# Handing work between engines at the seam of two stages, and splitting weights earlier in each unit of the last one

## The chip, the core and the metric

The kernel runs on one core of a Trainium2 chip. The metric is device time of one launch in microseconds, lower is better. Engines, as the profile names them: PE (TensorE matmul), DVE (VectorE), ACT (ScalarE), POOL (GpSimd), SP (the queue that starts most loads). Each engine works through its own list of instructions in order; semaphores tie the lists together.

## The reference

Three stages in one function: windowed attention, a mixture of 8 experts with the two best of each token, and a dense layer with a gated activation. All in float32; x has 1536 rows of 512.

```python
a = softmax(where(is_sink | in_window, q k^T / 8, -1e9));  x = a v       # 2 x 8 heads, 768 x 64
top2 = the two largest of x @ w_gate + softplus(x @ w_noise) * noise      # 8 experts
out[mask] += top2_w[mask, k, None] * (relu(x[mask] @ w1[e]) @ w2[e])      # 512 -> 1024 -> 512
h = x @ w_in                                                             # 512 -> 2048
sp = log1p(exp(h));  g = h * tanh(sp);  return g @ w_out                  # 2048 -> 512
```

## The kernel before

A float32 product is made of three fast products: each operand is split into a high part (`wh`, `xh`, `gh`) and the rest (`wl`, `xl`, `gl`), and PE adds high*high, high*rest and rest*high. A **split** of one 128x512 slice of weights is two instructions: ACT copies the staged slice to `wh` (L538), then POOL, or DVE if `lo='dve'` is given, subtracts it to make `wl` (L542). `Weights.split()` takes the next slice of a fixed list. Slices are loaded by SP into three staging buffers (`stg`); a subtraction that ends a staging buffer lets the next load start.

**Experts (`moe`).** For expert e, `l1` makes the hidden layer and `l2(e,b,half)` the output of row block b, in four blocks of two halves, with one split behind each half. An expert's rows go out to the table `yd`, and `gather(t,k)` fetches, with POOL's indirect DMA, the rows that belong to tile t of 128 tokens for choice k. Behind the last expert's halves the table `X2S` puts the **mixing** of the first four tiles: `x2a(t)` (L670, L671) scales the second gathered tile by its weight and adds the first times its own; both run on DVE, though `by='act'` sends the scaling to ACT (L669). `x2b(t)` transposes the mixed tile on PE (L676) and splits it into `xh` (ACT, L678) and `xl` (DVE, L679), the input of the last stage.

**Dense layer (`moe2`).** It runs in 48 units u: group g of 512 tokens, block f of 128 hidden columns. First come blocks 0 to 2 of group 0, each in two halves of 256 tokens; tiles 2 and 3 are transposed between the first half of block 0 and that of block 1 (`XH`). Then each unit holds, in this order: a mixing or a transposing of a later tile where the tables `XA2` and `XB2` name the unit (for the next group's tiles, so in units 0 to 31 only), `l1` (12 matmuls of 512 columns into `h`), the activation in three steps on three successive units as `MORD` says, one split in units 3 to 18 (`SPM`), a gather in even units, and `l2` of the block four units back (12 matmuls into the four banks of `o`).

The activation of block f: `mish_a` in unit f (ACT exponential L703; DVE L704, L705, L706; L706 is also the last reader of the PSUM tile `h`), `mish_b` in unit f+1 (ACT L709, L710, then the **gate**: POOL's product L711), `mish_c` in unit f+2 (ACT copy `gh` L715, DVE `gl` L716). The tiles `u` and `q` have three buffers, so unit u's exponential waits for `gl` of unit u-3. Block 3's `h` lies in a bank that the first `l2` needs as its fourth.

The order of the work is that of the code: no scheduler moves anything.

Of the kernel before, what the change touches and what calls it, by code (L numbers as in the profile page):

```python
# [467 lines left out]
    nc.scalar.activation(u,u,AF.Exp,scale=-1.0)  # L468
    nc.gpsimd.tensor_tensor(q,q,u,op=ALU.mult)
TX={(True,0,0): (0,),(True,0,1): (1,),(True,1,0): (2,),(True,2,0): (3,),(False,2,0): (0,1),(False,2,1): (2,3)}  # L470
X2S={(2,0):(lambda a,b: a(0),lambda a,b: a(1)),(3,0):(lambda a,b: b(0),lambda a,b: b(1),lambda a,b: a(2),lambda a,b: a(3))}
DS=4; LAG2=4; MB=3; GB=3; NH=3; XH=(0,0); SPM={u:1 for u in range(3,19)}; XA2=(1,5,9,12); XB2=(5,8,11,14); MORD=((0,0),(2,2),(1,1)); D_=512; FF=1024; F2=2048

class Weights:

# [71 lines left out]
def moe(ctx, tc, I, st, W, out, C=448, dbg=None, W32=None):  # L547
# [3 lines left out]
    pool=lambda name,bufs,**k: ph.enter_context(tc.tile_pool(name=name,bufs=bufs,reuse_waits="tile",**k))  # L551
# [19 lines left out]
    def l1(e,f,c0=0,c1=C,skip=0):  # L571

        xh,xl=XT[e]; n=4*e+f//4; wh,wl=W.hi[n],W.lo[n]; fs=slice(128*(f%4),128*(f%4)+128)
        p=bank['a'].tile([128,512],F32,name='a')
        w=c1-c0; i=0
        for k in range(4):
            for a,b in ((wh,xh),(wh,xl),(wl,xh)):
                nc.tensor.matmul(p[:,:w],a[:,k,fs],b[:,k,c0:c1],start=(i==0),stop=(i==11)); i+=1  # L578

        if c0==0: HH[f],HL[f]=one.tile([128,C+S],F32R,name=f'hh{f}'),one.tile([128,C-S],F32R,name=f'hl{f}')  # L580
        r=short(e); t=r+S
        for a,b in seg(c0+skip,c1,t): nc.scalar.activation(high(e,f,a,b),p[:,a-c0:b-c0],AF.Relu)
        for a,b in seg(c0+skip,c1,r,t):
            hl=HH[f][:,a+S:b+S] if r<=a<t else HL[f][:,a:b] if b<=r else HL[f][:,a-S:b-S]
            nc.vector.scalar_tensor_tensor(hl,p[:,a-c0:b-c0],0.0,high(e,f,a,b).bitcast(F32),op0=ALU.max,op1=ALU.subtract)  # L585
# [4 lines left out]
    def dbuf(t):  # L590
        if t<3: return dec.tile([128,256,2],U32,name='d64',bufs=3).rearrange("p n w -> p (n w)").bitcast(F32)
        return dec.tile([128,2,256],F32,name='dh').rearrange("p a n -> p (a n)")
    yw=st['yw']={}
    def l2(e,b,half):
        o,m=blocks(e)[b]
        if half==0: Y[0]=bank['c'].tile([128,512],F32,name='c')
        p=Y[0]
        two=0<m==S
        for f in range(4*half,4*half+4):
            n=4*e+2+f//4; wh,wl=W.hi[n][:,f%4,:],W.lo[n][:,f%4,:]  # L600
            if two:

                for i,w in enumerate((wh,wl)): nc.tensor.matmul(p[:2*m],HH[f][:,o:o+2*m],w,start=f+i==0,stop=f==7 and i==1)  # L603
            else:
                d=o-S if o>short(e) else o
                for i,(h,w) in enumerate(((high(e,f,o,o+m),wh),(high(e,f,o,o+m),wl),(HL[f][:,d:d+m],wh))): nc.tensor.matmul(p[:m],h,w,start=f+i==0,stop=f==7 and i==2)  # L606
        if half==1:
            s=yo.tile([128,512],F32,name='ys')
            if two:
                r=yo.tile([128,512],F32,name='ys')  # L610
                nc.scalar.activation(r[:m],p[m:2*m],AF.Copy)
                nc.vector.tensor_tensor(s[:m],p[:m],r[:m],op=ALU.add)
            else: nc.scalar.activation(s[:m],p[:m],AF.Copy)
            yw[e,b]=(nc.sync if (e,b)==(7,nb-1) else nc.scalar).dma_start(st['y'][e*C+o:e*C+o+m,:],s[:m])
# [17 lines left out]
    for e in range(8):  # L632
        if e: 
            
            for f in range(8):
                l1(e,f); W.split(); W.dstep(DS)
                if e<7 and f<nb: load_x(e+1,f)
                if e==7 and f>3: gather(f-4,0)
        for b in range(nb):
            if e==0 and b==LXB:  # L640
                for c in range(2,nb): load_x(0,c)
            if e==0 and b==2:
                
                for f in range(8):
                    l1(0,f,C-M,C,2*M-C); W.split(); W.dstep(2)
                    if f<nb: load_x(1,f)
            for half in range(2):
                l2(e,b,half)
                if e==0 and b==1 and half==0:
                    for c in range(2,nb): trans_x(0,c)  # L650
                if (e,half)==(7,1) and b<2: gather(2*b,1,dbuf(2*b)); gather(2*b+1,1,dbuf(2*b+1))
                W.split()
                if e==7:
                    for f in X2S.get((b,half),()): f(x2a,x2b)
                W.dstep(DS)
                for c in TX.get((e>0,b,half),()) if e<7 else (): trans_x(e+1,c)
# [25 lines left out]
def moe2(ctx, tc, I, st, W, out, C=448, dbg=None):  # L682
    nc=tc.nc; ident=st['ident']
    ph=ctx.enter_context(ExitStack())
    pool=lambda name,bufs,**k: ph.enter_context(tc.tile_pool(name=name,bufs=bufs,reuse_waits="tile",**k))
    xt=pool('n_x',1); gp=pool('n_g',GB); tp=pool('n_t',MB)
    ps_o=pool('np_o',4,space=PS); ps_h=pool('np_h',3,space=PS); ps_t=pool('np_t',1,space=PS)
    gather,x2a,x2b=st['gather'],st['x2a'],st['x2b']; X2=st['X2']; st['xt2'],st['ps_x2']=xt,lambda: (ps_t.tile([128,512],F32,name='xt') if O else ps_o.tile([128,512],F32,name='o')).rearrange("p (k q) -> p k q",k=4)
    G={}; HP={}; O={}

    e10=math.exp(10.0)
    def l1(g,f,c=slice(0,512)):
        xh,xl=X2[g]; n=32+f//4; wh,wl=W.hi[n],W.lo[n]; fs=slice(128*(f%4),128*(f%4)+128)
        if c.start==0: HP[g,f]=ps_h.tile([128,512],F32,name='h2') if (g,f)!=(0,3) else ps_o.tile([128,512],F32,name='o')
        p=HP[g,f]; i=0
        for k in range(4):
            for a,b in ((wh,xh),(wh,xl),(wl,xh)):
                nc.tensor.matmul(p[:,c],a[:,k,fs],b[:,k,c],start=(i==0),stop=(i==11)); i+=1  # L698
    Q={}
    def mish_a(g,f):  # L700
        p=HP.pop((g,f))
        u,q=[tp.tile([128,512],F32,name=n) for n in 'uq']; Q[g,f]=u,q
        nc.scalar.activation(u,p,AF.Exp)  # L703
        nc.vector.tensor_scalar(u,u,e10,None,op0=ALU.min)  # L704
        nc.vector.scalar_tensor_tensor(q,u,2.0,u,op0=ALU.add,op1=ALU.mult)  # L705
        nc.vector.tensor_tensor(u,p,q,op=ALU.mult)  # L706
    def mish_b(g,f):
        u,q=Q[g,f]
        nc.scalar.activation(q,q,AF.Ln,bias=st['two'])  # L709
        nc.scalar.activation(q,q,AF.Exp,scale=-1.0)  # L710
        nc.gpsimd.tensor_tensor(u,u,q,op=ALU.mult)  # L711
    def mish_c(g,f):
        u=Q.pop((g,f))[0]
        gh=gp.tile([128,512],F32R,name='gh'); gl=gp.tile([128,512],F32R,name='gl'); G[g,f]=(gh,gl)
        nc.scalar.activation(gh,u,AF.Copy)  # L715
        nc.vector.tensor_tensor(gl,u,gh.bitcast(F32),op=ALU.subtract)  # L716
    def l2(g,f):
        gh,gl=G.pop((g,f)); n=36+f//4; wh,wl=W.hi[n],W.lo[n]; k=f%4
        if f==0: O[g]=[ps_o.tile([128,512],F32,name='o') for _ in range(4)]
        for i in range(4):  # L720
            s=slice(128*i,128*i+128)
            for j,(a,w) in enumerate(((gh,wh),(gh,wl),(gl,wh))):
                nc.tensor.matmul(O[g][i],a[:,s],w[:,k,:],start=(f==0 and j==0),stop=(f==15 and j==2))  # L723
        if f==15:
            for i in range(4):
                if i%2==0: oo=W.spool.tile([128,2,512],F32,name='stg')
                o=oo[:,i%2,:]
                if i%2==0: nc.scalar.activation(o,O[g][i],AF.Copy)
                else: nc.vector.tensor_copy(o,O[g][i])
                r=512*g+128*i  # L730
                nc.sync.dma_start(out[r:r+128,:],o)
    
    gq=[(t,k) for t in range(4,12) for k in range(2)]
    for _ in range(2): gather(*gq.pop(0))
    for f in range(NH):
        l1(0,f,slice(0,256))
        for t in (2,3):
            if f==XH[t-2]: x2b(t)
    for f in range(NH): l1(0,f,slice(256,512))
    for u in range(48+LAG2):  # L740
        g,f=divmod(u,16)
        if g<2:
            if f in XA2: x2a(4*g+4+XA2.index(f))
            if f in XB2: x2b(4*g+4+XB2.index(f))
        if NH<=u<48: l1(g,f)
        for k,z in MORD:
            if 0<=u-k<48: (mish_a,mish_b,mish_c)[z](*divmod(u-k,16))
        if u<48:
            for i in range(SPM.get(u,0)): W.split(lo='dve' if i else 'pool')
            if f%2==0 and gq: gather(*gq.pop(0))  # L750
        if u>=LAG2: l2(*divmod(u-LAG2,16))
    ph.close()
# [79 lines left out]
```

## Time and profile before

| what | value |
|---|---|
| time, median of 3 runs | 748.19 us (747.0 to 750.71) |
| the profiled execution | 744.71 us, of which the span of the trace is 742.9 us |
| PE busy | 706.3 us, 95% |
| DVE busy | 491.1 us, 66% |
| ACT busy | 375.7 us, 51% |
| POOL busy | 352.3 us, 47% |
| chain that ended last | PE 64%, DVE 16%, DMA 6%, ACT 5% |

The last unit of the experts ends at about 459 us of the span, and the dense layer takes the rest, some 284 us. A busy share is an average over stages: what counts for an edit is where PE stood idle in the stretch that the edit touches, and which instruction released it.

### The profile page before, as it was taken

The page shows a single profiled execution, that of the slowest core. Times are in us where ns is not written, and L with a number is a line of the kernel's source. Part 1 is how long each engine was busy: PE and PEld are TensorE (multiplying, and loading weights), DVE is VectorE, ACT ScalarE, POOL GpSimd, SP SyncE. Part 2 cuts the span into 40 slices and gives each one's busy share as a digit, 9 for nine tenths or more (in the row PEclk, how much of TensorE's full clock was granted, in tenths as well). Part 3 has the DMA queues.
Part 4 walks back from the last instruction along what each step waited for, and adds up shares of the span by engine and source line. Part 5 has one row for each costly group of instructions (what it writes and reads, how often), then busy time and mean ns, then how long its engine had stood idle before and what let it go on. Part 6 is the DMA issues. An engine that isn't in the chain of part 4 may idle for free.

```text
span 742.9 us, 11343 instructions
## 1 busy us (share of the span) xinstructions
PE 706.3 (95%) x3888; PEld 591.1 (80%) x3888; DVE 491.1 (66%) x1099; ACT 375.7 (51%) x834; POOL 352.3 (47%) x321
## 2 busy tenths in 40 slices
PE   5998969999999999999999998999999999999996
PEld 4776658888788888989888886878778888888885
DVE  5778756588688788879876126689855655444442
ACT  5887633454454545545544443465545444444342
POOL 6236360575355445545445467366755442332321
PEclk9999979999999999999999999999999999999999
DMA  8995334587677778867867456212202100010001
GB/s 272 340 348 201 121 144 131 209 262 234 241 233 239 238 227 267 283 213 251 241 210 249 135 176 198 63 53 86 84 16 86 29 15 16 1 56 1 0 1 61
DMA packets 68336, 115.68 MB, mean 156 GB/s; under 512 B 6640, under 2 KB 20976, under 8 KB 68272
## 3 DMA queue, kind: packets, MB, share of 16 engines
q1 hardware_dynamic: 59424, 94.48, 39.2%
q0 software_dynamic: 3840, 12.59, 4.9%
q10 hardware_dynamic: 5008, 7.83, 3.0%
q8 instruction: 32, 0.52, 0.3%
q14 instruction: 32, 0.26, 0.1%
HBM read 82.36 MB, written 32.51 MB: 155 GB/s over the span
## 4 chain that ended last, share of the span: by engine, by line
PE 64%; DVE 16%; DMA 6%; ACT 5%; issue 3%; POOL 3%; another core or an unknown queue 1%; ACTq 1%; SPq 0%; POOLq 0%; DVEq 0%
PE o L723 15%; PE a L578 14%; PE h L698 14%; PE c L606 13%; ACT p L97 3%; PE c L603 2%; DMA wi<-dh 2%; DVE q L705 2%; DVE dh L508 2%; DVE dh L510 1%; PE a L94 1%; PE a L560 1%; POOL xg L212 1%; DVE gl L716 1%; DVE dh L506 1%
## 5 line engine op out<-in xcount | busy, mean ns | idle before, releaser
L542 POOL TENSOR_TENSOR wl<-stg,wh 128x512 fp32r<-128x512 f32 x156 | 206.4, 1335 | 171.7 <-ACT wh L538 160.6
L711 POOL TENSOR_TENSOR u<-u,q 128x512 f32<-128x512 f32 x48 | 79.0, 1645 | 146.6 <-DVE u L706 95.8
L538 ACT ACTIVATE wh<-stg 128x512 fp32r<-128x512 f32 x160 | 99.4, 625 | 39.9 <-DMA stg<-in_w_dram 12.3
L578 PE MATMUL a<-xl,wh 128*128 128x448 f32 (+1 forms) x288 | 100.1, 348 | 0.6 <-DVE xl L562 0.6
L578 PE MATMUL a<-xh,wh 128*128 128x448 f32 (+1 forms) x288 | 100.1, 348 | 0.0
L578 PE MATMUL a<-xh,wl 128*128 128x448 f32 (+1 forms) x288 | 99.9, 347 | 0.0
L703 ACT ACTIVATE u<-h 128x512 f32<-128x512 f32 x47 | 28.1, 598 | 121.4 <-PE h L698 101.7
L704 DVE TENSOR_SCALAR u<-u 128x512 f32<-128x512 f32 x48 | 22.2, 462 | 95.9 <-ACT u L703 95.8
L606 PE MATMUL c<-wh,hh 128*128 128x512 f32 x192 | 77.7, 405 | 0.0
L723 PE MATMUL o<-wl,gh 128*128 128x512 f32 x192 | 75.3, 392 | 1.7 <-POOL wl L542 1.6
L698 PE MATMUL h<-xh,wh 128*128 128x512 f32 (+1 forms) x200 | 76.9, 384 | 0.0
L606 PE MATMUL c<-wh,hl 128*128 128x512 f32 x192 | 75.5, 393 | 1.5 <-DVE hl L585 1.5
L723 PE MATMUL o<-wh,gl 128*128 128x512 f32 x192 | 74.9, 390 | 1.3 <-DVE gl L716 1.3
L698 PE MATMUL h<-xh,wl 128*128 128x512 f32 (+1 forms) x200 | 76.0, 380 | 0.0
L698 PE MATMUL h<-xl,wh 128*128 128x512 f32 (+1 forms) x200 | 76.0, 380 | 0.0
L723 PE MATMUL o<-wh,gh 128*128 128x512 f32 x192 | 74.9, 390 | 0.7 <-DVE u L706 0.7
L606 PE MATMUL c<-wl,hh 128*128 128x512 f32 x192 | 74.8, 390 | 0.0
L506 DVE TENSOR_SCALAR dh<-dh 128x256 f32<-128x256 f32 x64 | 41.6, 650 | 35.9 <-ACT dh L504 35.9
L504 ACT ACTIVATE dh<-d 128x256 f32<-128x256 f32 x64 | 27.6, 431 | 65.8 <-DMA wo<-dh 28.3
L578 PEld LDWEIGHTS a<-xl,wh 128*128 128x128 f32 x288 | 54.3, 189 | 4.7 <-DVE xl L562 1.2
L578 PEld LDWEIGHTS a<-xh,wh 128*128 128x128 f32 x288 | 54.3, 189 | 3.5
L578 PEld LDWEIGHTS a<-xh,wl 128*128 128x128 f32 x288 | 54.3, 189 | 3.3
(182 smaller groups left out, 1454.1 us busy)
## 6 DMA issues: line engine op xcount, KB each, us to landing
stg<-in_w_dram SPq DMA_DIRECT2D x64, 512.0 KB
d<-in_w_in_dram SPq DMA_DIRECT2D x32, 256.0 KB
d<-in_w_out_dram SPq DMA_DIRECT2D x32, 256.0 KB
xg<-zero SPq DMA_DIRECT2D x8, 896.0 KB
xr<-xg SPq DMA_DIRECT2D x24, 256.0 KB
yd<-ys ACTq DMA_DIRECT2D x23, 256.0 KB
wi<-dh SPq DMA_DIRECT2D x32, 128.0 KB
wo<-dh SPq DMA_DIRECT2D x32, 128.0 KB
```

Source lines behind the costliest of these rows:

```text
L97: nc.scalar.activation(o,tt[:,:n],AF.Exp,bias=NB[t][:,h:h+1],scale=-1.0,accum_out=RS[t][:,h:h+1])
L504: nc.scalar.activation(h,H,AF.Abs,scale=65536.0)
L506: h=T[i][1]; nc.vector.tensor_scalar(h,h,lo,hi,op0=ALU.max,op1=ALU.min)
L538: if hi=='act': s.nc.scalar.activation(h,src,AF.Copy)
L542: (s.nc.gpsimd if lo=='pool' else s.nc.vector).tensor_tensor(s.lo[n][:,j,:],s.stg[n,j//2][:,j%2,:],s.hi[n][:,j,:].bitcast(F32),op=ALU.subt ...
L578: nc.tensor.matmul(p[:,:w],a[:,k,fs],b[:,k,c0:c1],start=(i==0),stop=(i==11)); i+=1
L606: for i,(h,w) in enumerate(((high(e,f,o,o+m),wh),(high(e,f,o,o+m),wl),(HL[f][:,d:d+m],wh))): nc.tensor.matmul(p[:m],h,w,start=f+i==0,stop= ...
L698: nc.tensor.matmul(p[:,c],a[:,k,fs],b[:,k,c],start=(i==0),stop=(i==11)); i+=1
L703: nc.scalar.activation(u,p,AF.Exp)
L704: nc.vector.tensor_scalar(u,u,e10,None,op0=ALU.min)
L711: nc.gpsimd.tensor_tensor(u,u,q,op=ALU.mult)
L723: nc.tensor.matmul(O[g][i],a[:,s],w[:,k,:],start=(f==0 and j==0),stop=(f==15 and j==2))
```

## The change

Five things change, all between the last expert's third row block and the end of unit 31. (1) The four splits behind the last expert's blocks 2 and 3 make their `wl` on DVE instead of POOL. (2) Tiles 2 and 3 are scaled by ACT instead of DVE. (3) The first mixing of each group moves from unit 1 to unit 4 of the group, the second from 5 to 6. (4) The first transposing moves from unit 5 to 6. (5) In each unit the split is written ahead of the activation's steps instead of behind them; the gather keeps its place behind both.

```diff
-X2S={(2,0):(lambda a,b: a(0),lambda a,b: a(1)),(3,0):(lambda a,b: b(0),lambda a,b: b(1),lambda a,b: a(2),lambda a,b: a(3))}
-DS=4; LAG2=4; MB=3; GB=3; NH=3; XH=(0,0); SPM={u:1 for u in range(3,19)}; XA2=(1,5,9,12); XB2=(5,8,11,14); MORD=((0,0),(2,2),(1,1)); D_=512; FF=1024; F2=2048
+X2S={(2,0):(lambda a,b: a(0),lambda a,b: a(1)),(3,0):(lambda a,b: b(0),lambda a,b: b(1),lambda a,b: a(2,'act'),lambda a,b: a(3,'act'))}
+DS=4; LAG2=4; MB=3; GB=3; NH=3; XH=(0,0); SPM={u:1 for u in range(3,19)}; XA2=(4,6,9,12); XB2=(6,8,11,14); MORD=((0,0),(2,2),(1,1)); D_=512; FF=1024; F2=2048
@@ moe, behind each half of l2
-                W.split()
+                W.split(lo='dve' if e==7 and b>1 else 'pool')
@@ moe2, in each unit
         if NH<=u<48: l1(g,f)
+        if u<48:
+            for i in range(SPM.get(u,0)): W.split(lo='dve' if i else 'pool')
         for k,z in MORD:
             if 0<=u-k<48: (mish_a,mish_b,mish_c)[z](*divmod(u-k,16))
         if u<48:
-            for i in range(SPM.get(u,0)): W.split(lo='dve' if i else 'pool')
             if f%2==0 and gq: gather(*gq.pop(0))
```

At the seam, on DVE, before (`d_5286` and `d_5288` are the second rows of tiles 0 and 1, `d_5318` and `dh` those of tiles 2 and 3; `xl<-a` belongs to tiles 0 and 1, `xl<-o` to tiles 2 and 3):

```order
L612 TENSOR_TENSOR ys<-c,ys 64x512
L670 TENSOR_SCALAR d_5286<-d_5286,wB 128x512
L671 SCALAR_TENSOR_TENSOR xr<-xr,wA,d_5286 128x512
L670 TENSOR_SCALAR d_5288<-d_5288,wB 128x512
L671 SCALAR_TENSOR_TENSOR xr<-xr,wA,d_5288 128x512
L679 TENSOR_TENSOR xl<-a,xh 128x4x128 x2
L670 TENSOR_SCALAR d_5318<-d_5318,wB 128x512
L671 SCALAR_TENSOR_TENSOR xr<-xr,wA,d_5318 128x512
L670 TENSOR_SCALAR dh<-dh,wB 128x512
L671 SCALAR_TENSOR_TENSOR xr<-xr,wA,dh 128x512
L679 TENSOR_TENSOR xl<-o,xh 128x4x128 x2
```

and now:

```order
L612 TENSOR_TENSOR ys<-c,ys 64x512
L542 TENSOR_TENSOR wl_5340<-stg,wh_5339 128x512
L670 TENSOR_SCALAR d_5286<-d_5286,wB 128x512
L671 SCALAR_TENSOR_TENSOR xr<-xr,wA,d_5286 128x512
L670 TENSOR_SCALAR d_5288<-d_5288,wB 128x512
L671 SCALAR_TENSOR_TENSOR xr<-xr,wA,d_5288 128x512
L542 TENSOR_TENSOR wl_5340<-stg,wh_5339 128x512 x2
L679 TENSOR_TENSOR xl<-a,xh 128x4x128 x2
L671 SCALAR_TENSOR_TENSOR xr<-xr,wA,d_5318 128x512
L671 SCALAR_TENSOR_TENSOR xr<-xr,wA,dh 128x512
L542 TENSOR_TENSOR wl_5340<-stg,wh_5339 128x512
L679 TENSOR_TENSOR xl<-o,xh 128x4x128 x2
```

Four subtractions came to DVE, one of them ahead of the first mixing and two ahead of the first `xl`, and the two scalings of tiles 2 and 3 went to ACT.

On POOL from the same seam into unit 3, before (`wl4_5268` is the split just ahead of the four, `wl2_5340` the four, `wl5_5597` that of unit 3, under another number below; `u<-u,q` is the gate's product of blocks 0, 1 and 2, `xr<-yd` a gather):

```order
L666 DMA dh_5320<-yd_89,sloty_86 128x512
L542 TENSOR_TENSOR wl4_5268<-stg_5250,wh4_5267 128x512
L542 TENSOR_TENSOR wl2_5340<-stg_5292,wh2_5339 128x512 x2
L542 TENSOR_TENSOR wl2_5340<-stg_5324,wh2_5339 128x512 x2
L666 DMA xr_5443<-yd_89,sloty_86 128x512
L666 DMA xr_5445<-yd_89,sloty_86 128x512
L666 DMA xr_5542<-yd_89,sloty_86 128x512
L711 TENSOR_TENSOR u_5536<-u_5536,q_5537 128x512
L711 TENSOR_TENSOR u_5546<-u_5546,q_5547 128x512
L666 DMA xr_5568<-yd_89,sloty_86 128x512
L711 TENSOR_TENSOR u_5555<-u_5555,q_5556 128x512
L542 TENSOR_TENSOR wl5_5597<-stg_5364,wh5_5596 128x512
```

and now:

```order
L666 DMA dh_5320<-yd_89,sloty_86 128x512
L542 TENSOR_TENSOR wl4_5268<-stg_5250,wh4_5267 128x512
L666 DMA xr_5443<-yd_89,sloty_86 128x512
L666 DMA xr_5445<-yd_89,sloty_86 128x512
L666 DMA xr_5542<-yd_89,sloty_86 128x512
L711 TENSOR_TENSOR u_5536<-u_5536,q_5537 128x512
L711 TENSOR_TENSOR u_5544<-u_5544,q_5545 128x512
L666 DMA xr_5566<-yd_89,sloty_86 128x512
L542 TENSOR_TENSOR wl5_5582<-stg_5364,wh5_5581 128x512
L711 TENSOR_TENSOR u_5553<-u_5553,q_5554 128x512
```

The four subtractions are gone from between the gathers, and unit 3's stands ahead of block 2's product instead of behind it, as each unit's does up to unit 18.

On DVE in units 0 and 1, before (`h_5447` and `h_5474` are the PSUM tiles of blocks 0 and 1, `xr` the two gathered halves of tile 4):

```order
L705 SCALAR_TENSOR_TENSOR q<-u 128x512
L706 TENSOR_TENSOR u<-h_5447,q 128x512
L670 TENSOR_SCALAR xr<-xr,wB 128x512
L671 SCALAR_TENSOR_TENSOR xr<-xr,wA 128x512
L704 TENSOR_SCALAR u<-u 128x512
L705 SCALAR_TENSOR_TENSOR q<-u 128x512
L706 TENSOR_TENSOR u<-h_5474,q 128x512
```

and now:

```order
L705 SCALAR_TENSOR_TENSOR q<-u 128x512
L706 TENSOR_TENSOR u<-h_5447,q 128x512
L704 TENSOR_SCALAR u<-u 128x512
L705 SCALAR_TENSOR_TENSOR q<-u 128x512
L706 TENSOR_TENSOR u<-h_5474,q 128x512
```

The pair of tile 4's mixing left the place between blocks 0 and 1; it stands in unit 4 now, behind `gl` of block 1.

## Rows read from the trace of the kernel before

**Rows 1.** PE's waits from 455 us to the end: us in total, times, longest.

```profile
PE o L676 <- DVE xr L671: 3.0, 2, 2.4
PE o L723 <- POOL wl L542: 1.6, 2, 1.2
PE o L723 <- DVE gl L716: 1.3, 1, 1.3
PE o L723 <- DVE u L706: 0.7, 1, 0.7
```

**Rows 2.** Busy time by stretch, PE alone: length, busy (count), granted clock, DMA share, GB/s.

```profile
464.90:468.31 3.41, 3.41 (x19) 0.50 0.79 253
```

**Rows 3.** PE's timeline at the seam: start, length, instruction, idle before it.

```profile
455.52 1.03 PE L676 MATMUL a<-ident,xr 128*128 128x128 f32 x8
...
459.15 0.28 PE L698 MATMUL h<-xh,wh 128*128 128x256 f32 x1
...
460.46 0.28 PE L698 MATMUL h<-xh,wl 128*128 128x256 f32 x1
...
473.55 0.40 PE L698 MATMUL o<-xh,wh 128*128 128x512 f32 x1
```

**Rows 4.** DVE's timeline at the seam.

```profile
453.66 0.75 DVE L671 SCALAR_TENSOR_TENSOR xr<-xr,wA,d 128x512 f32<-128x512 f32 x1
456.81 1.29 DVE L679 TENSOR_TENSOR xl<-a,xh 128x512 fp32r<-128x512 f32 x2 [2.40 <-ACT xh L678]
458.01 4.26 DVE L670 TENSOR_SCALAR d<-d,wB 128x512 f32<-128x512 f32 x1
```

**Rows 5.** POOL's timeline at the seam.

```profile
454.76 0.95 POOL L666 DMA_INDIRECT dh<-yd,sloty  x1 [0.30 <-issue]
455.73 6.25 POOL L542 TENSOR_TENSOR wl<-stg,wh 128x512 fp32r<-128x512 f32 x5
```

**Rows 6.** DMA issues from 444 to 535 us: count, us to landing.

```profile
dh<-yd,sloty POOLq DMA_INDIRECT x1, 3.8
```

**Rows 7.** ACT's timeline at the seam.

```profile
456.19 1.07 ACT L678 ACTIVATE xh<-a 128x512 fp32r<-128x512 f32 x2
459.35 0.60 ACT L613 ACTIVATE ys<-c 128x512 f32<-128x512 f32 x1 [2.09 <-PE c L606]
```

**Rows 8.** DVE's timeline in units 0 to 3.

```profile
473.36 0.48 DVE L670 TENSOR_SCALAR xr<-xr,wB 128x512 f32<-128x512 f32 x1
...
479.36 1.55 DVE L716 TENSOR_TENSOR gl<-u,gh 128x512 fp32r<-128x512 f32 x1
481.63 0.43 DVE L704 TENSOR_SCALAR u<-u 128x512 f32<-128x512 f32 x1 [0.72 <-ACT u L703]
...
482.82 0.69 DVE L706 TENSOR_TENSOR u<-o,q 128x512 f32<-128x512 f32 x1
```

**Rows 9.** POOL's timeline there.

```profile
479.09 1.27 POOL L711 TENSOR_TENSOR u<-u,q 128x512 f32<-128x512 f32 x1 [2.84 <-ACT q L710]
```

**Rows 10.** DVE's timeline in units 8 and 9.

```profile
513.44 3.61 DVE L705 SCALAR_TENSOR_TENSOR q<-u 128x512 f32<-128x512 f32 x1
...
517.69 0.68 DVE L716 TENSOR_TENSOR gl<-u,gh 128x512 fp32r<-128x512 f32 x1
```

**Rows 11.** POOL's timeline in units 8 to 11.

```profile
513.95 1.30 POOL L711 TENSOR_TENSOR u<-u,q 128x512 f32<-128x512 f32 x1
515.20 1.29 POOL L542 TENSOR_TENSOR wl<-stg,wh 128x512 fp32r<-128x512 f32 x1
...
525.61 1.30 POOL L711 TENSOR_TENSOR u<-u,q 128x512 f32<-128x512 f32 x1
526.86 1.26 POOL L542 TENSOR_TENSOR wl<-stg,wh 128x512 fp32r<-128x512 f32 x1
```

**Rows 12.** PE's timeline in units 11 and 12.

```profile
521.61 0.39 PE L723 MATMUL o<-wh,gl 128*128 128x512 f32 x1
...
528.17 0.50 PE L723 MATMUL o<-wl,gh 128*128 128x512 f32 x1 [1.19 <-POOL wl L542]
```

## The prediction

> **What bounds the kernel now.** I read the busy shares first (PE 95%), then who PE waits for from the edited stretch on, then the timelines round each wait. From 455 us to the end PE waits only six times, for four kinds of release [rows 1]: 3.0 us for the mixed tiles 2 and 3 at the seam, 1.6 for a split's subtraction on POOL, 1.3 for a `gl` and 0.7 for the L706 that frees block 3's bank. All else in the dense layer is PE at its own pace, so an edit here can win no more than these waits and what they drag behind them.
>
> At the seam the first half of block 0 issues its last matmul at 460.46, and block 3 starts at 473.55 [rows 3]. In between lie 60 matmuls of 256 columns and 8 transposes. The pace of such a matmul is (460.46 - 459.15) / 11 = 0.119 us, and eight transposes took 1.03 [rows 3]: 7.1 + 1.0 = 8.2 us of work, with 0.12 for the last issue. The gap is 13.1. So the seam costs 4.8 us, not the 3.0 that the waits show: after the idle time the granted clock stood at 0.50 for 3.41 us, the lower of its two levels (1.2 GHz) [rows 2], and work at half speed for so long loses half of it, 1.7. Why PE waited: DVE's scaling of tile 2 began at 458.01 and took 4.26 us, where the same instruction took 0.48 elsewhere [rows 4, 8]. POOL ran five subtractions without a pause from 455.73 to 461.98 [rows 5], and the scaling ended 0.3 after that run. DVE stood still while POOL worked.
>
> **The change part by part.** *Term A, the seam.* Four of POOL's five subtractions go to DVE and both scalings to ACT. POOL's run then ends near 455.73 + 1.25 = 456.98 (a fifth of 6.25 [rows 5]). I place DVE's new list as badly as the rows allow. Its subtraction is not in the trace; bounds are half of the `xl` pair, 0.65, and an L671, 0.75 [rows 4]; I take 0.69 as for the other two-operand L706 [rows 8]. The first subtraction pushes the mixing of tile 1 from its end, 454.41, to 455.10 at the latest; PE transposes it at 455.52 [rows 3, 4], so this is covered by 0.4. The next two: the second may be held until 456.98, ends 457.67, the third 458.36, the `xl` pair 459.65 (was 458.10). Block 0's second matmul reads that `xl` at 459.27, so up to 0.4 us of waiting is new. ACT takes the scaling of tile 2 behind its `xh` pair, which ends at 457.26, and that of tile 3 when the rows land, 454.76 + 3.8 = 458.56 [rows 5 to 7]; ACT's price for 128x512 is 0.53 (half the pair) to 0.60 [rows 7]. Both are done by 459.2, before the copy of the expert's last block that stands behind them could start anyway, 459.35 [rows 7]. DVE then needs two L671 at 0.75: tiles 2 and 3 are ready at 460.4 and 461.15, when PE has finished block 0 (some 460.9 with the new wait) and tile 2's transposes (461.4). The idle time goes, and with it, I expect, the clock's fall: the shorter waits of [rows 1] left no such stretch. The fourth subtraction needs the last `wh` and runs while PE transposes. A = 4.8 less 0 to 0.4; I take 4.6. Lower bound 0.6: only the second, shorter wait (3.0 - 2.4) goes, and the clock falls as now.
>
> *Term B, units 0 to 4.* The mixing of tile 4 leaves the place between blocks 0 and 1 on DVE: an L670 and an L671, 0.48 + 0.75 = 1.23 [rows 4, 8], in a row in which DVE had work up to the late `gl` that PE waited for. All that hangs on it (`gl` of block 0, then block 3's exponential, then L704 and L706 [rows 8]) comes 1.23 earlier. The two waits are one chain of 2.0 us, since the second is set by an L706 three steps behind that `gl`; so B = +1.2, with 0.8 left as a wait. Two things may move it. `gl` is held 0.9 us (1.55 against 0.68 [rows 8, 10]) by block 1's product [rows 9]: if it slips in before, all goes and B = +2.0. Against it, unit 3's subtraction now stands ahead of block 2's product, right behind a gather and ready early; if it and that product hold L704 in turn, that is 1.29 + 1.30 [rows 11], and B = 1.2 - 2.6 = -1.4. ACT's copy for the split now stands ahead of the exponential and could meet a load that is not there yet, which would hold the whole activation behind it; loads run three staging buffers ahead and the seam's earlier subtractions free theirs sooner, so I cost it at nothing.
>
> In unit 4 the mixing comes back. There DVE stood idle 0.72 before each L704 while ACT took the exponential [rows 8], so some 0.5 of the 1.23 lands on DVE's path. The gathers that reuse its buffer stand behind block 3's product on POOL, later than the mixing. The cover for DVE being late is what PE leaves it: `gl` of block 7 ends at 518.37 and is read at 521.61 [rows 10, 12], 3.2 us. After B takes 1.2 and the mixing 0.5 of it, 1.5 is left, so I cost it at nothing. The units above 16 have no stall to win and idle engines: nothing.
>
> *Term C, the late splits.* Two `l2` waited 1.6 for a subtraction on POOL [rows 1], the larger 1.19 [rows 12]. The row of POOL shows why: the subtraction at 526.86 stood behind the product of 525.61 [rows 11], which waits for DVE and ACT. Now it stands ahead of it: 1.30 sooner by the product's length alone, against 1.19, and the second wait was 1.6 - 1.2 = 0.4. PE also comes 1.2 earlier by B, but the product's own wait for its operands is spared too. C = 1.6. If ACT's copy for the split comes no sooner than now, only the product's length is won and PE's advance eats it: lower bound 1.30 - 1.2 = 0.1.
>
> *A rule against the rows.* When a DVE instruction is held, the rows show it held through whole runs: 4.26 us at the seam past three more subtractions, and an L705 of 3.61 that ended 0.56 after a product and a subtraction behind it (515.20 + 1.29) [rows 4, 5, 10, 11]. The Trainium skill (SBUF — State Buffer, Who interferes with whom) says that DVE with two SBUF inputs and a GpSimd instruction that reads SBUF exclude each other, and that the one issued second waits for the first to finish. The trace agrees on the exclusion, not on the length. By the rule B's bad case would be 1.2 - 1.3 = -0.1 instead of -1.4, and the sum of the lower ends that much better. The rule also speaks against giving DVE four more such instructions while POOL still has subtractions.
>
> *Sum.* 4.6 + 1.2 + 1.6 = 7.4. The profiled execution would take 744.71 - 7.4 = 737.3. It lies 3.5 below the median of the runs, 748.19; I lay the same gain on the median: 740.8.
>
> **The rivals.** (1) *DVE is held by one POOL instruction at a time.* Then `gl` of block 0 gets in between product and subtraction, both waits of B go, and B = 2.0: 748.19 - (4.6 + 2.0 + 1.6) = 740.0. For it: that `gl` was held for one product only [rows 8, 9]. Against it: the two long rows. The rule of the Trainium skill above is this mechanism. (2) *Only the seam.* The earlier subtraction gives DVE back its waits in another place; B and C cancel. 748.19 - 4.6 = 743.6. For it: POOL's work in units 3 to 18 is not less than before, only in another order. (3) *The seam's wait stays*: ACT's scalings or DVE's held subtractions come 2 us later than placed, PE waits as long as now and the clock falls. A = 0.6: 748.19 - (0.6 + 1.2 + 1.6) = 744.8. For it: the margins above are 0.3 to 0.5 us. Against it: I placed them late already. (4) *Slower: DVE becomes the bound in units 4 to 18.* The subtraction now runs while DVE is at the activation's two-operand steps, and each pair of units costs DVE both of its subtractions, 2 x 1.29 [rows 11], more than before. Over 7 pairs that is 18.1, less the 3.2 of cover: 14.9 lost against A + C = 6.2, so 748.19 + 8.7 = 756.9. It decides when a pair costs more than (6.2 + 3.2) / 7 = 1.3 us, one subtraction. For it: L705 held 3.61. Against it: before, too, each pair had two of them in the same stretch, and nothing was added there but one mixing.
>
> **How the numbers follow.** Forecast 0.45, (1) 0.20, (2) 0.18, (3) 0.10, (4) 0.07. The likeliest is 740.8. Best case: 4.8 + 2.0 + 1.6 = 8.4, 739.8, and the runs before lie up to 1.2 below their median: low 738.6, which I set at 738.4. At the other end the range takes in (2) and (3), 744.8, and 0.6 for the spread of the runs: high 745.4; outside are (4) and the worst of the others. A measurement of this kernel can tell some 0.5%, 3.7 us, from no change: faster means below 744.4. That holds the forecast, (1) and two thirds of (2): 0.45 + 0.20 + 0.13 = 0.78. Same: the rest of (2) and (3), 0.15. Slower: (4), 0.07.
>
> **What would show it.** A: no wait of PE on an L671 above 0.5 us at the seam, and no stretch at half clock between the seam and the end of block 2; DVE's L670 of 4 us gone. B: PE's waits on L716 and L706 in the first `l2` together below 1 us. C: no wait of PE on L542. Rival (4) would show as new waits of PE on `gl` in units 5 to 18. The prediction is wrong if PE's waits go and the time does not, or if the clock falls at the seam without a wait.

## The result

The changed kernel takes 739.84 us (median of 6 runs, 737.25 to 742.87) against 749.45 us for the kernel before on the same chips (6 runs, 746.98 to 752.5). The ratio on record is 0.9886, with an interval of 0.985 to 0.9921: 1.1% faster, which in us is 5.9 to 11.2. The forecast was 740.8 us, its range 738.4 to 745.4.

The profiled execution of the changed kernel spans 738.1 us, only 4.8 less than the one before. That difference mixes two things, for the stages ahead of the edited code move by several microseconds from execution to execution. So I measure PE in three stretches. **S1** runs from block 0's first matmul (the seam) to the first `l2`, **S2** is the first `l2`, **S3** goes from there to the last run of 60 `l2` matmuls (to 0.16 us behind the start of its first matmul, in every trace alike). The seam lies at 459.15 in the trace before [rows 3] and at 463.65 in the one after. The columns of both views are the stretch, its length, PE's busy time and count of instructions, the granted clock, the share of the DMA engines and GB/s. Before, PE by stretch:

```profile
459.15:479.01 19.86, 16.86 (x105) 0.91 0.38 124
479.01:484.36 5.35, 3.29 (x13) 1.00 0.18 49
484.36:722.73 238.37, 236.63 (x1054) 1.00 0.10 34
```

After, the same stretches:

```profile
463.65:479.09 15.44, 15.23 (x106) 1.00 0.50 169
479.09:482.46 3.37, 3.00 (x13) 1.00 0.21 39
482.46:717.69 235.23, 235.23 (x1054) 1.00 0.11 35
```

The work is the same to within a lost record: in S3 it is 1054 matmuls both times. S1 lost 4.42 us and its granted clock rose from 0.91 to 1.00, S2 lost 1.98, S3 3.14, and PE has no idle time left there. Together that is 9.54. The tails behind the last run, 20.17 and 20.41, take 0.24 back, so the dense layer is 9.30 us shorter; the medians differ by 9.61. PE's waits from the seam on are these two, where there were six [rows 1]; the columns are us in total, times, longest:

```profile
PE o L723 <- DVE u L706: 0.4, 1, 0.4
PE h L698 <- DVE xl L679: 0.2, 1, 0.2
```

At the seam, DVE's new row in the profile after (start, length, instruction, idle time before it and what ended it):

```profile
459.50 0.69 DVE L542 TENSOR_TENSOR wl<-stg,wh 128x512 fp32r<-128x512 f32 x1
460.84 2.05 DVE L542 TENSOR_TENSOR wl<-stg,wh 128x512 fp32r<-128x512 f32 x1 [0.66 <-ACT wh L538]
462.81 1.27 DVE L679 TENSOR_TENSOR xl<-a,xh 128x512 fp32r<-128x512 f32 x2
464.01 0.73 DVE L671 SCALAR_TENSOR_TENSOR xr<-xr,wA,d 128x512 f32<-128x512 f32 x1
464.67 0.74 DVE L671 SCALAR_TENSOR_TENSOR xr<-xr,wA,dh 128x512 f32<-128x512 f32 x1
```

The scaling of 4.26 us [rows 4] is gone from DVE. The subtraction at 460.84 is held for 1.36 us by the one that POOL kept:

```profile
461.02 1.31 POOL L542 TENSOR_TENSOR wl<-stg,wh 128x512 fp32r<-128x512 f32 x1
```

This makes the first `xl` late, and PE waits 0.21 us for it at its second matmul:

```profile
463.65 0.28 PE L698 MATMUL h<-xh,wh 128*128 128x256 f32 x1
464.14 0.39 PE L698 MATMUL h<-xl,wh 128*128 128x256 f32 x1 [0.21 <-DVE xl L679]
```

Two of the four subtractions on DVE were held in this way. The first of them, ahead of the mixing, stands behind the two that POOL ran before:

```profile
455.15 2.06 DVE L542 TENSOR_TENSOR wl<-stg,wh 128x512 fp32r<-128x512 f32 x1 [1.77 <-ACT wh L538]
```

```profile
454.12 2.53 POOL L542 TENSOR_TENSOR wl<-stg,wh 128x512 fp32r<-128x512 f32 x2
```

The mixed tiles 2 and 3 are ready at 465.4, and their transposes at 465.56 start without a wait.

### The profile page after: what moved, and what is told of

It is laid out like the page before. It is cut to its first block, busy times and chain, and to the rows that moved or that the text cites. A ratio compares the mean times of both kernels' runs of the same rounds, so it can differ in the third digit from the quotient of the medians.

```text
span 738.1 us, 11346 instructions
## 1 busy us (share of the span) xinstructions
PE 709.0 (96%) x3888; PEld 597.0 (81%) x3888; DVE 494.4 (67%) x1101; ACT 376.6 (51%) x836; POOL 347.0 (47%) x317
## 4 chain that ended last, share of the span: by engine, by line
PE 79%; DVE 5%; DMA 5%; ACT 4%; POOL 4%; issue 2%; ACTq 0%; SPq 0%; POOLq 0%; DVEq 0%
PE a L578 19%; PE o L723 17%; PE h L698 17%; PE c L606 15%; PE c L603 3%; POOL xg L212 2%; ACT p L97 2%; PE a L94 2%; PE a L560 2%; PE a L104 1%; PE c L116 1%; DMA wi<-dh 1%; DMA xr<-xg 1%; POOL wl L542 1%; DMA qp<-in_qP_dram 1%
## 5 line engine op out<-in xcount | busy, mean ns | idle before, releaser
L542 POOL TENSOR_TENSOR wl<-stg,wh 128x512 fp32r<-128x512 f32 x152 | 202.3, 1342 | 173.3 <-ACT wh L538 163.8
L711 POOL TENSOR_TENSOR u<-u,q 128x512 f32<-128x512 f32 x48 | 77.3, 1610 | 138.2 <-DVE u L706 94.8
L538 ACT ACTIVATE wh<-stg 128x512 fp32r<-128x512 f32 x160 | 99.3, 626 | 41.2 <-DMA stg<-in_w_dram 10.0
L704 DVE TENSOR_SCALAR u<-u 128x512 f32<-128x512 f32 x48 | 28.1, 584 | 88.4 <-ACT u L703 88.2
L506 DVE TENSOR_SCALAR dh<-dh 128x256 f32<-128x256 f32 x64 | 47.2, 738 | 34.7 <-ACT dh L504 34.1
```

What stands on the lines that cost most here:

```text
L506: h=T[i][1]; nc.vector.tensor_scalar(h,h,lo,hi,op0=ALU.max,op1=ALU.min)
L538: if hi=='act': s.nc.scalar.activation(h,src,AF.Copy)
L542: (s.nc.gpsimd if lo=='pool' else s.nc.vector).tensor_tensor(s.lo[n][:,j,:],s.stg[n,j//2][:,j%2,:],s.hi[n][:,j,:].bitcast(F32),op=ALU.subt ...
```

## Experiments

The stretches of all runs, each read as above. The expectation for the seam alone names 3.53 and 235.07 for the changed kernel's S2 and S3: there the border between the two lay 0.16 us later, and the sum is the same.

| kernel | seam at | S1 | S2 | S3 |
|---|---|---|---|---|
| before | 459.15 | 19.86 | 5.35 | 238.37 |
| before, again | 458.38 | 19.86 | 5.36 | 238.25 |
| changed | 463.65 | 15.44 | 3.37 | 235.23 |
| changed, again | 462.15 | 15.42 | 3.39 | 235.26 |
| seam only | 461.25 | 15.42 | 5.35 | 238.31 |
| units only | 461.33 | 18.36 | 3.38 | 235.23 |
| subtractions on DVE only | 462.21 | 16.05 | 5.37 | 238.22 |
| scalings on ACT only | 462.04 | 16.12 | 5.40 | 238.27 |
| tables only | 460.52 | 19.22 | 3.37 | 236.26 |
| split ahead only | 459.72 | 19.81 | 6.68 | 235.20 |
| five subtractions on DVE | 461.77 | 15.95 | 3.38 | 235.22 |
| memset between | 464.91 | 15.46 | 3.38 | 239.78 |

### Do the stretches repeat?

The kernel before and the changed one were run once more, with no edit.

> The kernel before, unchanged, once more. Theory: S1, S2 and S3 repeat within 0.3 us of 19.86, 5.35 and 238.37, and the seam's start (459.15 before, 463.65 after) moves by several us from execution to execution, as the attention stage is not touched by the change. Rival: the seam's start is at 459 again and the changed kernel's 463.65 is an effect of the change.

> The changed kernel, unchanged, once more. Theory: S1, S2 and S3 repeat within 0.3 us of 15.44, 3.37 and 235.23, so that the stretches tell more than the whole time does; the seam's start lies anywhere between 458 and 464 us. Rival: they move by more than 0.5 us, and the readings of the single runs at that size mean nothing.

All three stretches repeat within 0.12 us. The seam's start does not: it went from 459.15 to 458.38 and from 463.65 to 462.15, and the kernel before has the earlier one both times. PE's rows settle whether the change did that. The last block of the last expert but one (its first matmul of L603), ahead of all edited code, starts at 415.19 in the kernel before and at 419.70 in the changed one. From there to the seam both take 43.95 us, as do the other ten traces (43.94 to 43.95). So the 4.5 us by which the changed kernel's seam lies later arose ahead of the change. The whole times of the kernel before spread by more than 10 us in 19 runs; how much of this is the part ahead of the seam is known for the traced ones alone. From here on single executions are compared by stretches, and times only where there are several runs.

### The seam alone

Against the kernel before:

```diff
-                W.split()
+                W.split(lo='dve' if e==7 and b>1 else 'pool')
-X2S={(2,0):(lambda a,b: a(0),lambda a,b: a(1)),(3,0):(lambda a,b: b(0),lambda a,b: b(1),lambda a,b: a(2),lambda a,b: a(3))}
+X2S={(2,0):(lambda a,b: a(0),lambda a,b: a(1)),(3,0):(lambda a,b: b(0),lambda a,b: b(1),lambda a,b: a(2,'act'),lambda a,b: a(3,'act'))}
```

> Only the two edits at the seam: four subtractions on DVE, the scalings of tiles 2 and 3 on ACT; tables and the order in the units as before. I measure three stretches of PE: S1 from block 0's first matmul to the first l2 (19.86 us before, 15.44 after), S2 the first l2 (5.35 and 3.53), S3 from there to the start of the last run of l2 matmuls (238.37 and 235.07). Theory (the seam and the units are separate): S1 15.4 to 15.6, no half clock at the seam; S2 5.3 and S3 238.4 as before; time 4.4 us below the kernel before, 745.0 on a median of 749.5. Rival (what the seam wins, the units give back, since DVE and POOL are as busy there as before): S1 falls to 15.4, S2 + S3 grow by 2 us or more, time within 2.5 us of before.

S1 is 15.42, S2 and S3 are those of before. The time is 743.07 us (10 runs) against 747.55 (19 runs), ratio 0.9955, interval 0.9921 to 0.9989. The medians lie 4.5 us apart; the interval, 0.8 to 5.9 us, takes in the 4.44 of S1 but can't confirm it closely. Nothing is given back later in S2 and S3; the rival falls.

### The units alone

```diff
-... XA2=(1,5,9,12); XB2=(5,8,11,14); ...
+... XA2=(4,6,9,12); XB2=(6,8,11,14); ...
+        if u<48:
+            for i in range(SPM.get(u,0)): W.split(lo='dve' if i else 'pool')
         for k,z in MORD:
             if 0<=u-k<48: (mish_a,mish_b,mish_c)[z](*divmod(u-k,16))
         if u<48:
-            for i in range(SPM.get(u,0)): W.split(lo='dve' if i else 'pool')
```

> Only the edits in the units: later mixing and transposing, and the split ahead of the activation; the seam as before. Theory: the wait of 2.4 us on the mixing and the half clock at the seam stay, S1 19.9; S2 3.5 to 4.1, S3 235.1 to 236; time 5.1 us below before, 744.3. Rival (the units gain only because the seam is repaired and DVE starts earlier): S1 19.9, S2 and S3 at 5.3 and 238, time as before.

S2 and S3 are those of the changed kernel, and the time is 742.13 us (10 runs) against 747.55, ratio 0.9944, interval 0.992 to 0.9967, that is 2.5 to 6.0 us. By the stretches the two halves are separate and add up: 4.44 at the seam, 1.97 + 3.14 in the units.

S1 missed: 18.36 where 19.9 was expected. PE's waits at the seam are to the hundredth those of before (2.37 and 0.62), but the clock stayed up. PE's wait, and PE by stretch over all of S1 (the middle window is that of [rows 2], though this seam lies 2.2 us later):

```profile
465.29 0.66 PE L676 MATMUL o<-ident,xr 128*128 128x128 f32 x4 [2.37 <-DVE xr L671]
```

```profile
461.33:464.90 3.57, 1.59 (x13) 1.00 0.75 241
464.90:468.31 3.41, 2.40 (x19) 1.00 0.83 281
468.31:479.69 11.38, 11.38 (x76) 1.00 0.16 49
```

So of the 4.4 us of the seam the half clock is 1.5 (19.86 - 18.36), which does not follow each time, and what the waits cost is the rest, 2.9.

### Which of the two edits at the seam?

First only the subtractions go to DVE (the `W.split` line above), then only the scalings to ACT (the `X2S` line).

> At the seam only the four subtractions go to DVE; the scalings stay on DVE, the units as before. Theory (POOL's unbroken run of five subtractions held DVE): with the run gone the scaling takes 0.48 and the mixing of tile 3 ends 2 x 0.48, some 1 us later than in the changed kernel, so PE waits some 0.6 to 1.0 us for it without a fall of the clock: S1 16.0 to 16.6. Rival (DVE has too much to do at the seam and the scalings had to leave it): DVE's row grows by 4 x 0.69, S1 at 18 or more, with a wait above 2 us on L671.

> At the seam only the two scalings go to ACT; POOL keeps its run of five subtractions, the units as before. Theory: the first L671 has two inputs in SBUF and is held in place of the scaling until POOL's run ends, so it takes some 4 us; only the 2 x 0.5 us of the scalings are won: S1 18.5 to 19.4, and a wait of PE on L671 of 1.5 us or more, most likely with the clock's fall. Rival (the scaling's own kind of instruction was what POOL held): S1 15.4 to 15.8, L671 at 0.75.

The subtractions alone give 16.05, inside the forecast: the scaling that took 4.26 takes 0.47, PE waits 0.45 us for tile 3, which the two scalings on DVE make later, and no fall of the clock follows. DVE's row and PE's:

```profile
462.55 0.47 DVE L670 TENSOR_SCALAR d<-d,wB 128x512 f32<-128x512 f32 x1
```

```profile
465.14 0.63 PE L676 MATMUL o<-ident,xr 128*128 128x128 f32 x4 [0.45 <-DVE xr L671]
```

This is the run that shows the cause: the same instruction in the same place on DVE is not held once POOL's run is gone. The scalings alone give 16.12, which neither forecast had. DVE's and POOL's rows of that kernel:

```profile
461.49 2.73 DVE L671 SCALAR_TENSOR_TENSOR xr<-xr,wA,d 128x512 f32<-128x512 f32 x1 [0.31 <-ACT d L669]
464.14 0.74 DVE L671 SCALAR_TENSOR_TENSOR xr<-xr,wA,dh 128x512 f32<-128x512 f32 x1
```

```profile
458.63 5.04 POOL L542 TENSOR_TENSOR wl<-stg,wh 128x512 fp32r<-128x512 f32 x4
464.99 1.28 POOL L542 TENSOR_TENSOR wl<-stg,wh 128x512 fp32r<-128x512 f32 x1 [1.32 <-ACT wh L538]
```

L671 is held as the theory says: it ends 0.55 us after POOL's run. But the run is one subtraction shorter. ACT now waits for the rows of tile 3 ahead of the last split's copy, so POOL's fifth subtraction comes 1.32 us after the fourth, and DVE gets its turn there. That is a side effect of ACT's order that my expectation had left out. The rival is refuted by the held L671, though S1 came out nearer to its number. Either edit alone wins 3.7 to 3.8 us, both together 4.4; in all three the clock stays up, so up to 1.5 of each is the half clock, which can stay away without any edit.

Would the fifth subtraction on DVE win the 0.21 us that PE still waits?

```diff
-                W.split(lo='dve' if e==7 and b>1 else 'pool')
+                W.split(lo='dve' if e==7 and (b>1 or b==1 and half==1) else 'pool')
```

> The changed kernel, with the fifth subtraction (behind block 1's second half) on DVE too. Theory: the third DVE subtraction, which took 2.05 us while POOL ran that fifth one, takes 0.69, the first xl pair is ready in time and PE's wait of 0.21 us for it and its slow restart go: S1 15.1, S2 and S3 3.5 and 235.1. Rival (the subtraction was held by the two gathers): S1 15.4 with the third subtraction still at 2 us.

The subtraction in question takes 0.69 as expected and the wait for `xl` is gone, yet S1 is 15.95: now tile 2's rows land later, and both scalings with them, and PE waits 0.48 for L671. DVE's row, then ACT's:

```profile
459.16 0.69 DVE L542 TENSOR_TENSOR wl<-stg,wh 128x512 fp32r<-128x512 f32 x1 [0.26 <-ACT wh L538]
```

```profile
462.28 0.72 ACT L669 ACTIVATE d<-d,wB 128x512 f32<-128x512 f32 x1 [2.17 <-DMA d<-yd,sloty]
462.93 0.72 ACT L669 ACTIVATE dh<-dh,wB 128x512 f32<-128x512 f32 x1
```

Neither forecast. The gather had been issued at 455.95, some 6.3 us ahead of the scaling, where the changed kernel has 4.3 (457.88 to 462.14); why it took longer was not tried.

### Which of the two edits in the units?

First the tables alone, then the split ahead of the activation alone.

> Only the later mixing and transposing (tables XA2 and XB2); seam and order in the units as before. Theory (the mixing between blocks 0 and 1 made the first gl late): S2 3.5 to 4.2 with the wait on gl gone; S3 as before, 238 to 239, since POOL still makes each split behind the product, so the wait of 1.2 us on L542 stays; S1 19.9. Rival (the gain in S2 comes from POOL's new order): S2 5.3.

> Only the split ahead of the activation's steps; seam and tables as before. Theory: PE's waits on L542 are gone and S3 falls to 235 to 236; S2 stays at 5.3 or grows to 8, as unit 3's subtraction now holds DVE where the mixing still sits between blocks 0 and 1. Rival (the late split was due to DVE's lateness, not to its place on POOL): S3 237.5 or more.

The tables alone give all of S2, 3.37. In S3 they were to give nothing and gave 2.11: no wait on L542 is left in the list, though by the starts of the matmuls four `l2` still have a late second one, 1.0 us together. That DVE, and with it POOL's product ahead of each split, comes earlier without the backlog between blocks 0 and 1 fits this, but was not tried apart. S1, expected at 19.9, was 19.22: the half clock began at 464.22, ahead of the transposes at 464.48, and covered most of the second wait (0.16 instead of 0.62). The split ahead alone gives all of S3, 235.20, and costs 1.33 in S2. PE's waits of that kernel:

```profile
PE o L676 <- DVE xr L671: 3.0, 2, 2.4
PE o L723 <- DVE u L706: 2.0, 1, 2.0
PE o L723 <- DVE gl L716: 1.3, 1, 1.3
```

The 2.0 is the bad case that the prediction had named: unit 3's subtraction runs just when block 3's L704 comes, and holds it (DVE's row, then POOL's):

```profile
482.14 1.75 DVE L704 TENSOR_SCALAR u<-u 128x512 f32<-128x512 f32 x1 [0.72 <-ACT u L703]
```

```profile
482.30 1.30 POOL L542 TENSOR_TENSOR wl<-stg,wh 128x512 fp32r<-128x512 f32 x1
```

So the split ahead of the activation needs the tables: alone it wins 3.17 and gives 1.33 back.

### How long does POOL hold DVE?

```diff
-    Q={}
+    Q={}; gap=xt.tile([128,1],F32,name='gap')
@@ moe2, in each unit
+            if u in SPM: nc.gpsimd.memset(gap,0.0)
             for i in range(SPM.get(u,0)): W.split(lo='dve' if i else 'pool')
+            if u in SPM: nc.gpsimd.memset(gap,0.0)
```

> The changed kernel with a POOL memset of one column ahead of and behind each of the sixteen splits in units 3 to 18. It asks how long POOL holds DVE. In the changed kernel the gl of block 1 takes 3.84 us, while POOL runs subtraction, product and subtraction without a gap. Theory (DVE is held as long as POOL's instructions that read SBUF follow each other without a gap): the small write breaks the row, no L716 or L705 in units 3 to 18 takes over 2.2 us; PE hardly waits now, so S2 and S3 stay at 3.4 and 235.2 and the time with them. Rival (what holds DVE is that the instruction began behind a gather, or that it must come to rest behind all that POOL has taken up): holds above 3 us stay.

The long hold stays, so a small write between POOL's readers doesn't let DVE in:

```profile
482.81 3.94 DVE L716 TENSOR_TENSOR gl<-u,gh 128x512 fp32r<-128x512 f32 x1
```

S3 is 239.78, 4.5 more, and not by waits: PE is busy throughout, at a granted clock of 1.00. Its `l2` runs of 12 matmuls take 2.80 us instead of 2.72 to the end, long past the last memset, and of `l1` only those of group 1 do (546 to 637 us); groups 0 and 2 stay at 2.73. Those are the runs that read tiles of the pool to which the edit added `gap` (`xh` and `xl` of group 1) or of the pool opened next (`gh`, `gl`), which points to where the tiles lie and not to the memsets; no run has `gap` without them. S2 and S1 were as in the changed kernel.

The traces show one condition of the long holds, which this run did not change. In the kernel before, between 445 and 575 us, five DVE instructions were held in a run of two or more POOL instructions that had begun within 0.1 us behind a gather, and all five were held to the end of the run, such as the L705 of 3.61 [rows 10, 11]. Five were held in runs that had begun otherwise, and all five got in between. One of these, DVE's row and POOL's:

```profile
487.90 1.29 DVE L716 TENSOR_TENSOR gl<-u,gh 128x512 fp32r<-128x512 f32 x1
```

```profile
487.34 1.30 POOL L711 TENSOR_TENSOR u<-u,q 128x512 f32<-128x512 f32 x1 [0.64 <-POOL wl L542]
488.60 1.74 POOL L542 TENSOR_TENSOR wl<-stg,wh 128x512 fp32r<-128x512 f32 x1
```

Over all twelve traces it is 46 of 46 held to the end behind a gather, and 61 of 61 let in between elsewhere. No run moves a gather alone, so that the gather is the cause is not shown.

## Why the prediction was right

**The seam, A = 4.6, measured 4.42.** The mechanism held: POOL's run kept DVE out, and with the run gone PE has no wait on L671. The placing came out, in part by other steps than those it names. The first subtraction did not take 0.69 but 2.06, held by POOL's two before it; it delayed the mixing of tile 1 by only 0.67, measured against the seam, since in the kernel before the scaling of tile 0 had been held there in its stead:

```profile
450.72 1.72 DVE L670 TENSOR_SCALAR d<-d,wB 128x512 f32<-128x512 f32 x1 [1.84 <-DMA d<-yd,sloty]
```

That the 0.4 us of cover was enough is luck in so far as the text had not priced that hold. POOL's last subtraction held the third on DVE, not the second, and PE's wait of up to 0.4 us came out as 0.21. The prices were near where nothing was held: 0.68 to 0.69 for a subtraction on DVE (taken 0.69), 0.73 for a scaling on ACT (taken 0.53 to 0.60). Two things the prediction did not see. The half clock is not bound to the wait: behind the same wait of 2.37 us it came in four executions and not in a fifth. And the edits overlap, each doing most of the work alone.

**Units 0 to 4, B = 1.2, measured 1.98.** Mis-sized in its value, though the text names the case that came: the first `gl` slipped in ahead of block 1's product. DVE's row and POOL's in the changed kernel, the latter held in its turn:

```profile
478.04 0.68 DVE L716 TENSOR_TENSOR gl<-u,gh 128x512 fp32r<-128x512 f32 x1
```

```profile
478.34 1.53 POOL L711 TENSOR_TENSOR u<-u,q 128x512 f32<-128x512 f32 x1 [2.02 <-ACT q L710]
```

It had 0.3 us to spare; in the kernel before, `gl` began 0.27 after the product and was held [rows 8, 9]. That it comes so near the 2.0 of that case is partly chance: PE still waits 0.4 for L706, and the first `l2`, 2.72 at its pace, loses 0.65 where it lost 2.63 before, more than the 2.0 listed. That POOL's earlier subtraction can cost here was right too, and shows once the mixing is left in its old place. In unit 4 the mixing costs PE nothing, as priced.

**The late splits, C = 1.6, measured 3.14.** This step was mis-sized by half. It added up the waits that the list names. In the kernel before, five `l2` and not two had a late second matmul, the one that reads `wl`; at those two the list says 1.6, but the gap is longer by the pace that PE takes to restart, and three more gaps are too short for the list. Two of the three, where a matmul should follow after 0.227:

```profile
545.65 0.39 PE L723 MATMUL o<-wh,gh 128*128 128x512 f32 x1
545.96 0.50 PE L723 MATMUL o<-wl,gh 128*128 128x512 f32 x1
546.29 0.39 PE L723 MATMUL o<-wh,gl 128*128 128x512 f32 x1
...
556.75 0.39 PE L723 MATMUL o<-wh,gh 128*128 128x512 f32 x1
557.25 0.50 PE L723 MATMUL o<-wl,gh 128*128 128x512 f32 x1
557.59 0.40 PE L723 MATMUL o<-wh,gl 128*128 128x512 f32 x1
```

The first loses 0.08 and 0.10, the second 0.27 and 0.11. Summed over the five by matmul starts it is 2.9 of the 3.14. The place on POOL was not the whole cause either: the tables alone win 2.11 of it, the split ahead alone 3.17.

**The rivals.** (1), with 740.0, came nearest in time, but not by its mechanism. A `gl` of the changed kernel was held through subtraction, product and subtraction, and ended 0.56 after the third (484.80):

```profile
481.52 3.84 DVE L716 TENSOR_TENSOR gl<-u,gh 128x512 fp32r<-128x512 f32 x1
```

```profile
481.04 1.29 POOL L542 TENSOR_TENSOR wl<-stg,wh 128x512 fp32r<-128x512 f32 x1
482.27 1.29 POOL L711 TENSOR_TENSOR u<-u,q 128x512 f32<-128x512 f32 x1
483.52 1.28 POOL L542 TENSOR_TENSOR wl<-stg,wh 128x512 fp32r<-128x512 f32 x1
```

The Trainium skill (SBUF — State Buffer, Who interferes with whom) has the second of two such instructions wait for the first to finish; here DVE waited for three, and the measurement decides; the `gl` at 487.90 above waited for one. (2), the seam only, and (3), the seam's wait stays, are refuted by S2 and S3 and by S1. (4), DVE becomes the bound, is refuted by the two waits that are left: DVE is still held for long in units 3 to 18, but PE's lead covers it. My sum was 7.4 and the stretches gave 9.5; B was too small by the order in which one `gl` and one product began, C because a late instruction costs PE more than the wait that is listed for it. The time came out closer than the sum did, 739.84 against 740.8, because the gain was taken off 748.19, the median of three runs, and the six of the result have 749.45: that 1.3 us is luck.

## What to carry to other kernels

Where one engine stands still beside another, see whether it is held by a whole run or by a single instruction, look for an indirect DMA directly ahead of the run, and take work out of the run: four subtractions moved off POOL's row ended the hold, while taking the held instruction off DVE passed the hold on to the next one (2.73 us) and helped because the run became shorter. Price a wait on PE by the gap between the starts of its matmuls, not by the wait that is listed: restarting and short waits made term C here nearly twice as large. An edit that moves work earlier can need a second one to be worth its price, so try the parts alone before keeping or dropping them.

## What the hardware showed beside that

The clock after a wait: PE's wait of 2.37 us at the seam was followed by a stretch at half clock in the kernel before, both times, and in the two kernels with the tables or the split's place alone, but not in the kernel with both of them, where S1 was 1.5 us shorter. A scaling of 128x512 by a column took ACT 0.72 to 0.73 us, against 0.60 for a plain copy of that size from PSUM [rows 7] and 0.62 to 0.64 for one from SBUF (L538). DVE's instruction that was let in first held POOL's next one as well: a product of 1.29 us took 1.53 (at 478.34 above) behind the `gl` that had begun 0.3 us earlier.
